# A linear-attention and Mish feed-forward kernel: the first feed-forward product by one level of Strassen's method, in two passes over DFF, with a written order on every engine

## The chip, the cores and the metric

The kernel runs on one core of a Trainium2 chip. The metric is device time in microseconds (us) of one execution, the median of several. Engines: PE (TensorE, matrix products), DVE (VectorE), ACT (ScalarE), POOL (GpSimd), and SP, whose queue issues all DMA transfers here.

## The reference

```python
def phi(x):
    proj = np.einsum('bhsd,df->bhsf', x, w_phi)
    proj = proj - np.max(np.abs(proj), axis=-1, keepdims=True)
    return np.concatenate([np.exp(proj), np.exp(-proj)], axis=-1)
q_p, k_p = (phi(q), phi(k))
kv = np.einsum('bhsf,bhsd->bhfd', k_p, v)
z = np.sum(k_p, axis=2)
num = np.einsum('bhsf,bhfd->bhsd', q_p, kv)
den = np.einsum('bhsf,bhf->bhs', q_p, z)[..., None] + 1e-06
attn_out = num / den
x = attn_out.transpose(0, 2, 1, 3).reshape(B * S, H * D)
h = x @ w_in
g = h * np.tanh(log1p(exp(h)))
out = g @ w_out
```

Batch 8, 8 heads, 576 positions, head width 64, 128 features; so x has 4608 tokens (rows) of DM = 512, and DFF = 2048. All is float32; `w_in` and `w_out` arrive as float64 words, of which the kernel makes float32 pairs.

## The kernel before, in words

**Attention.** The work is cut into 36 units of 512 rows each for k and for q. For a unit of k: a DMA brings it (`k_load`, L131), PE projects it (`project`, L103, 16 matmuls), DVE takes the largest magnitude of each row and subtracts it (L112, L113), ACT takes two exponentials (L147, L148), PE sums the products with v into PSUM (`k_sum`, L150), and ACT copies finished sums out (L163). For a unit of q: the same projection and subtraction, then PE transposes (`q_turn`, L176), ACT takes the exponentials out of PSUM (L182), PE multiplies with the sums of k (`q_num`, L184), DVE divides (L198 to L200), PE transposes back (`q_out`, L203), ACT copies (L211) and a DMA writes x to DRAM (`x_spill`, L212). k runs three units ahead of q (`LEAD`).

**Feed-forward.** Each float32 operand is split into a high part that PE's float32r format holds exactly and a low part; a product is three matmuls (high by high, high by low, low by high). x comes in 18 chunks of 256 tokens. A tile is 128 of DFF for one chunk: `ff_in` (L231) makes 12 matmuls of 128x256 (4 blocks of DM by 3), ACT applies Mish to two tiles at once (L251) and casts the high part (`gh`, L254), DVE subtracts for the low part (`gl`, L255), and `ff_out` (L259) makes 6 matmuls of 128x512 into two PSUM banks. There are 18 x 16 = 288 tiles.

**Weights.** They are split in 32 pieces of 128x512 by `split_weight` (L78): one ACT operation for the magnitude (L87), seven DVE operations (L89 to L94, L99, L100) and one ACT cast (L98). Sixteen pieces are split beside the attention and sixteen after it. The first four chunks are worked with half of DFF at a time (`NSPLIT`), so that the second sixteen have time.

**Order.** Each step is put in a list with a due time (`at`, L292) and emitted in order of these times. Inside `tc.manual_schedule(engines={PE})` (L343) only PE keeps the order of emission; the other engines and the DMA queue are put in order by a scheduler. `table` (L60) ties the ACT operations that need an activation table to each other. PSUM: `ps_a` holds two tiles of two banks (projections, later `h`), `ps_b` four tiles of one bank.

Of the kernel before, what the change touches and what calls it, by code (L numbers as in the profile page):

```python
# [38 lines left out]
def attention_then_mish(ctx, tc, qT, kT, va, w_phi, w_in, w_out, out):  # L39
# [18 lines left out]
    last = None

    def table(act):  # L60

        nonlocal last
        if last is not None:
            tc.add_manual_dep(act.ins, last.name, mybir.DependencyInfo(mybir.DependencyClass.NoSync, mybir.DependencyReason.DATA),
                              reason="table")
        last = act.ins


    weight, words_of = {}, {}

    def load_weight(pool, kind, i, j):
        nm = f"{kind}_{i}_{j}"
        src = w_in[i * P:(i + 1) * P, j * 512:(j + 1) * 512] if kind == "in" else w_out[i * P:(i + 1) * P, :]
        words = pool.tile([P, 1024], U32, tag=f"w{nm}", name=f"words_{nm}", bufs=1)
        nc.sync.dma_start(words, src.bitcast(U32))
        words_of[kind, i, j] = words.rearrange("p (a b) -> p a b", b=2)

    def split_weight(pool, kind, i, j):  # L78


        nm = f"{kind}_{i}_{j}"
        words = words_of.pop((kind, i, j))
        low, high = words[:, :, 0], words[:, :, 1]
        w = ffn.tile([P, 512], U32, tag="u", name=f"w_{nm}", bufs=3)
        t = ffn.tile([P, 512], F32, tag="t", name=f"t_{nm}", bufs=2)
        wf = w.bitcast(F32)
        nc.scalar.activation(wf, high.bitcast(F32), AF.Abs)  # L87

        nc.vector.tensor_scalar(wf, wf, LARGE, SMALL, op0=ALU.min, op1=ALU.max)  # L89
        nc.vector.tensor_scalar(w, w, 3, 0x3FFFFFF8, op0=ALU.logical_shift_left, op1=ALU.bitwise_and)  # L90
        nc.vector.scalar_tensor_tensor(w, high, 0xC0000000, w, op0=ALU.bitwise_and, op1=ALU.bitwise_or)

        nc.vector.tensor_scalar(t.bitcast(U32), w, 0xFF800000, None, op0=ALU.bitwise_and)
        nc.vector.scalar_tensor_tensor(t, low, 2.0 ** -52, t, op0=ALU.mult, op1=ALU.mult)  # L94
        parts = pool.tile([P, 2, 512], F32R, tag=f"w{nm}", name=f"parts_{nm}", bufs=1)
        hi, lo = parts[:, 0, :], parts[:, 1, :]
        weight[kind, i, j] = (hi, lo)
        nc.scalar.copy(hi, wf)  # L98
        nc.vector.tensor_sub(wf, wf, hi.bitcast(F32))  # L99
        nc.vector.tensor_tensor(lo, wf, t, op=ALU.add)  # L100


    def project(raw, name):  # L103

        ps = ps_a.tile([P, 2, 4, F], F32, tag="pp", name=f"pp_{name}")
        for n in range(4):
            for j in range(2):
                rows = slice(j * D, (j + 1) * D)
                nc.tensor.matmul(ps[:, j, n], raw[rows, n * P:(n + 1) * P], w_phi2[rows], start=True, stop=True)  # L109
# [34 lines left out]

    def k_exp(n):
        e = k_live[n]
        table(nc.scalar.activation(e[:, :, 1, :], e[:, :, 0, :], AF.Exp))  # L147
        table(nc.scalar.activation(e[:, :, 0, :], e[:, :, 0, :], AF.Exp, scale=-1.0))  # L148

    def k_sum(n):  # L150
        es = k_live.pop(n)
        for i in range(4):
            for p, slot in pairs_of(4 * n + i):
# [7 lines left out]
                if slot == 4:  # L161
                    kv[p // NHP, p % NHP] = att.tile([P, 2, 2, VW], F32, tag="kv", name=f"kv_{p}", bufs=10)
                    nc.scalar.copy(kv[p // NHP, p % NHP], kv_ps.pop(p))  # L163
# [214 lines left out]
```

## Time and profile before

| | |
|---|---|
| median of 3 runs | 1198.48 us (1198.43 to 1201.16) |
| profiled execution | 1201.74 us, of which the span of the profile is 1200.0 us |
| busy in the span | PE 1122.3, DVE 471.0, ACT 458.7, POOL 0.7 us |
| mean granted PE clock | 0.974 |
| DMA traffic | 78.43 MB |

The profile is one execution. A row of its windows view gives, for a stretch of the span, the busy time of each engine with the number of its instructions, then the granted PE clock (1.00 is full speed), the share of the DMA engines and GB/s. A row of the groups gives a line of the kernel, engine and operation, output and input with shapes and count, the busy time and the mean of one in ns, and the idle time of the engine ahead of them with what ended it. A row of the timeline gives start, length, engine, line and operation.

### The profile page before, as it was taken

To read this page: it belongs to the slowest core of one execution; us is meant where nothing else is said; L and a number is where in the kernel's file an instruction comes from. 1 tells how busy PE (TensorE), PEld (TensorE's weight loads), DVE (VectorE), ACT (ScalarE), POOL (GpSimd) and SP (SyncE) were. 2 spreads that over 40 slices of the span, in tenths; PEclk is the share of its full clock that TensorE was granted. 3 is DMA by queue.
4 is the path that set the end of the run, shared out by engine and by line. 5 is a ranking of instruction groups with operands and counts; after the bars stand their busy time and mean duration, and the time that the engine had idled before them with its cause. 6 is when DMAs were issued, how large, how long until landed. Compare 5 with 4: busy or idle time off the path is not lost.

```text
span 1200.0 us, 25819 instructions
## 1 busy us (share of the span) xinstructions
PE 1122.3 (94%) x11632; PEld 1017.9 (85%) x11632; DVE 471.0 (39%) x772; ACT 458.7 (38%) x708; POOL 0.7 (0%) x6
## 2 busy tenths in 40 slices
PE   5548899999999878999999999999999999999998
PEld 5548788888889777999999999999999999999997
DVE  7997677777753777222111111111111111111111
ACT  4445555656554777222222222222222222222221
POOL 0000000000000000000000000000000000000000
PEclk8779999999999989999999999999999999999999
DMA  9314444443313500111010010010010010000000
GB/s 364 129 39 132 142 157 128 137 133 124 114 55 138 205 19 18 36 54 36 19 36 19 18 36 18 19 36 19 18 36 18 19 36 19 18 19 1 19 18 18
DMA packets 33373, 78.43 MB, mean 65 GB/s; under 512 B 3696, under 2 KB 3824, under 8 KB 33264
## 3 DMA queue, kind: packets, MB, share of 16 engines
q1 hardware_dynamic: 33264, 76.79, 18.7%
q8 instruction: 91, 1.49, 0.5%
q14 instruction: 18, 0.15, 0.0%
HBM read 57.90 MB, written 18.87 MB: 64 GB/s over the span
## 4 chain that ended last, share of the span: by engine, by line
PE 72%; DVE 19%; ACT 3%; DMA 3%; issue 2%; SPq 1%; DVEq 0%; ACTq 0%
PE h L243 32%; PE o L273 31%; PE dt L180 3%; DVE e_q L113 3%; DVE m_k L112 3%; DVE e_k L113 3%; PE pp_k L109 3%; DVE m_q L112 3%; DMA words_out<-w_out 2%; PE num L121 1%; DVE x L200 1%; ACT L251 1%; PE kvps L121 1%; DMA x<-x_spill 1%; PE pp_q L109 1%
## 5 line engine op out<-in xcount | busy, mean ns | idle before, releaser
L243 PE MATMUL h<-xTh,parts_in 128*128 128x256 f32 x2304 | 459.2, 284 | 15.0 <-ACT u L251 15.0
L243 PEld LDWEIGHTS h<-xTh,parts_in 128*128 128x128 f32 x2304 | 378.2, 192 | 28.7 <-ACT u L251 17.5
L273 PE MATMUL o<-parts_out,gh 128*128 128x512 f32 x1152 | 363.6, 397 | 0.0
L243 PE MATMUL h<-xTl,parts_in 128*128 128x256 f32 x1152 | 326.9, 284 | 0.0
L255 DVE TENSOR_TENSOR gl<-u,gh 128x512 fp32r<-128x512 f32 x144 | 99.5, 691 | 486.5 <-ACT gh L254 486.4
L251 ACT ACTIVATE u<-h 128x512 f32<-128x512 f32 x144 | 86.1, 598 | 517.2 <-PE h L243 517.1
L243 PEld LDWEIGHTS h<-xTl,parts_in 128*128 128x128 f32 x1152 | 221.1, 192 | 10.0
L273 PE MATMUL o<-parts_out,gl 128*128 128x512 f32 x576 | 224.8, 390 | 0.0
L273 PEld LDWEIGHTS o<-parts_out,gh 128*128 128x128 f32 x1152 | 201.2, 191 | 27.7
L273 PEld LDWEIGHTS o<-parts_out,gl 128*128 128x128 f32 x576 | 109.1, 189 | 24.9
L121 PE MATMUL kvps<-v,e_k 128*64 128x65 f32 x2560 | 87.6, 230 | 4.0 <-ACT e_k L148 4.0
L254 ACT CAST gh<-u 128x512 fp32r<-128x512 f32 x144 | 89.4, 621 | 3.8
L121 PEld LDWEIGHTS kvps<-v,e_k 128*64 128x64 f32 x2560 | 82.6, 145 | 9.1 <-ACT e_k L148 4.6
L182 ACT ACTIVATE e_q<-dt 128x512 f32<-128x512 f32 x144 | 74.7, 603 | 12.7 <-PE dt L180 12.3
L121 PE MATMUL num<-kv,e_q 128*64 128x65 f32 x2304 | 74.3, 221 | 0.8 <-ACT kv L163 0.7
L180 PE MATMUL dt<-ident,e_q 128*128 128x128 f32 x288 | 45.6, 286 | 29.4 <-DVE r L198 17.9
L121 PEld LDWEIGHTS num<-kv,e_q 128*64 128x64 f32 x2304 | 70.8, 137 | 1.7 <-ACT kv L163 0.8
L112 DVE TENSOR_REDUCE m_k<-pp_k 128x8 f32<-128x1024 f32 x36 | 44.1, 1225 | 61.1 <-PE pp_k L109 61.1
L180 PEld LDWEIGHTS dt<-ident,e_q 128*128 128x128 f32 x288 | 31.8, 144 | 41.2 <-PE xt L209 13.4
L147 ACT ACTIVATE e_k<-e_k 128x1024 f32<-128x1024 f32 x36 | 38.1, 1057 | 72.2 <-DVE e_k L113 72.2
L228 DVE TENSOR_TENSOR xTl<-x,xTh 128x1024 fp32r<-128x1024 f32 x22 | 27.0, 1226 | 96.9 <-ACT xTh L227 96.9
L109 PE MATMUL pp_k<-w_phi,kraw 64*128 64x128 f32 x576 | 48.4, 315 | 11.5 <-issue 7.4
...
## 6 DMA issues: line engine op xcount, KB each, us to landing
...
kraw<-kT SPq DMA_DIRECT2D x36, 256.0 KB, 2.7
qraw<-qT SPq DMA_DIRECT2D x36, 256.0 KB, 3.2
x_spill<-xs SPq DMA_DIRECT2D x36, 256.0 KB, 2.0
out<-osb SPq DMA_DIRECT2D x36, 256.0 KB, 2.0
...
```

What stands on the lines that cost most here:

```text
L109: nc.tensor.matmul(ps[:, j, n], raw[rows, n * P:(n + 1) * P], w_phi2[rows], start=True, stop=True)
L112: nc.vector.tensor_reduce(m, ps, axis=AX.X, op=ALU.max, apply_absolute_value=True)
L113: nc.vector.tensor_tensor(e[:, :, 0, :].rearrange("p j (n f) -> p j n f", f=F), ps, m.unsqueeze(3).broadcast_to([P, 2, 4, F]), op=ALU.subt ...
L121: nc.tensor.matmul(ps[rows], lhsT[:, rows], rhs[h], start=start, stop=stop, skip_group_check=True)
L147: table(nc.scalar.activation(e[:, :, 1, :], e[:, :, 0, :], AF.Exp))
L180: nc.tensor.transpose(ps[:, i * P:(i + 1) * P], e[:, 0, i * P:(i + 1) * P], ident)
L182: table(nc.scalar.activation(e[:, s, :], ps, AF.Exp, scale=2.0 * s - 1.0))
L243: nc.tensor.matmul(ps, w[:, wcol], x[:, cc, :], start=(n == 0), stop=(n == 11))
L251: table(nc.scalar.activation(u, hv, AF.Mish))
L254: nc.scalar.copy(gh.rearrange("p f s -> p (f s)"), u)
L255: nc.vector.tensor_sub(gl.rearrange("p f s -> p (f s)"), u, gh.rearrange("p f s -> p (f s)").bitcast(F32))
L273: nc.tensor.matmul(ps, g[:, cols], w, start=(i == first and k == 0), stop=(i == end and k == 2))
```

## The change

**Strassen.** x comes in 9 chunks of 512 tokens, DFF in 8 blocks of 256, so there are 72 steps (`steps`). For one step the first product is a 2x2 block product (two blocks of 128 of DFF, two halves of DM, two halves of the tokens). Winograd's form of Strassen's method makes it from seven block products in place of eight: 7 products x 2 blocks of 128 in DM x 3 = 42 matmuls of 128x256. Four sums of weight blocks are made once for each weight piece (`sums`, on DVE), four sums of x blocks for each chunk that is loaded (`x_sum`, on POOL), and the seven products are put together by DVE and ACT (`first_product`, `winograd`). The second product is as before: 24 matmuls of 128x512 for a step. `ff_in` is in two parts: four products, then three that go into or beside the same banks, after DVE and ACT have read what the first four left.

**Two passes.** DFF is worked in two halves. Of the 32 weight pieces 8 are split beside the attention and 24 during the feed-forward; those of the second half (`fp` 4 to 7) are written to DRAM when split and read back once the place of the first half is free (`again`, `again_out`). Partial outputs go to DRAM (`o_part`) and come back (`part_load`).

**Engines.** `gl` is made on POOL, but for the last step. After the attention the magnitude of a weight is taken on DVE (`quiet`), not on ACT. `tc.manual_schedule()` now keeps the written order on all engines and on the DMA queue; `table` is gone. Steps that were one function are cut (`k_center`, `k_store`, `q_exp`, `q_norm`, `q_store`) so that each engine's part has a due time of its own. k runs four units ahead.

```diff
+PRODUCTS = ((0, 0, 0, 0), (4, 1, 0, 1), (3, 2, 1, 0), (5, 3, 1, 1), (2, 4, 0, 0), (6, 5, 1, 0), (1, 6, 1, 1))
...
+    def weight_ops(kind, fp, k, quiet):
...
+            if quiet:
+                nc.vector.tensor_scalar(w().bitcast(U32), words[:, 1], 0x7FFFFFFF, None, op0=ALU.bitwise_and)
+            else:
+                nc.scalar.activation(w(), words[:, 1].bitcast(F32), AF.Abs)
...
+        def sums(i):
...
+            nc.vector.tensor_tensor(o, x, y, op=op)
+
+        def hi():
...
+            nc.scalar.copy(dst[:, 0], piece[key][1][:, 1:8] if kind == "in" else w())
+
+        def lo():
+            dst = piece[key][3]
+            nc.vector.tensor_sub(dst[:, 1], piece[key][1][:, 1:8], dst[:, 0].bitcast(F32))
+            done()
...
+            if fp >= HALF:
+                nc.sync.dma_start(in_spill[fp, k] if kind == "in" else out_spill[fp, k], dst.bitcast(F32))
...
+    def x_sum(s, i):
...
+        nc.gpsimd.tensor_tensor(o, a, b, op=ALU.subtract)
+
+    def x_block(s, b):
...
+        nc.scalar.copy(blk[:, 0], src)
+        nc.vector.tensor_sub(blk[:, 1], src, blk[:, 0].bitcast(F32))
...
+    def ff_in(n, which):
...
+        for i in range(4) if which == 0 else range(4, 7):
+            wb, xb, bank, half = PRODUCTS[i]
+            ps = h_live[n][:, bank, half]
...
+                for w, x in ((wh, xh), (wh, xl), (wl, xh)):
+                    nc.tensor.matmul(ps, w, x, start=(i in (0, 2) and m == 0), stop=(m == 5), skip_group_check=True)
...
+        nc.scalar.copy(p1, h_live[n][:, 0, 0])
...
+            nc.vector.tensor_tensor(u2, ps[:, 0, 1], u_live[n][0], op=ALU.add)
...
+            nc.vector.tensor_tensor(u4, ps[:, 1, 0], u_live[n][1], op=ALU.add)
...
+            nc.vector.tensor_tensor(u[:, 3], ps[:, 1, 1], u_live[n][2], op=ALU.add)
...
+            nc.vector.tensor_tensor(u[:, 1:3], ps[:, 1], u2.unsqueeze(1).broadcast_to([P, 2, CH]), op=ALU.add)
...
+            nc.scalar.activation(u[:, 0], h_live[n][:, 0, 0], AF.Mish)
...
+            nc.scalar.activation(u[:, 1:4], u[:, 1:4], AF.Mish)
...
+        nc.scalar.copy(gh, u_live[n][3])
...
+        eng = nc.vector if n == len(steps) - 1 else nc.gpsimd
+        eng.tensor_tensor(gl, u_live.pop(n)[3], g_live[n][0].bitcast(F32), op=ALU.subtract)
...
+    segs = [(sc, (0, 1)) for sc in range(NFIRST)] + [(sc, (2, 3)) for sc in range(NFIRST)]
+    segs += [(sc, (0, 1, 2, 3)) for sc in range(NFIRST, NSC)] + [(sc, (4, 5, 6, 7)) for sc in range(NSC)]
...
-    with tc.manual_schedule(engines={mybir.EngineType.PE}):
+    with tc.manual_schedule():
```

**Where instructions moved.** First, DVE early in the attention. `m` and `e` are the largest magnitude and the difference of a unit; `w_`, `t_`, `words_` and `parts_` belong to weight pieces, and the last number of a name is that of its buffer. Before:

```order
L99 TENSOR_TENSOR w_out_0_1191<-w_out_0_1191,parts_out_0_1199 128x512
L91 SCALAR_TENSOR_TENSOR w_out_0_1771<-words_out_0_1345,w_out_0_1771 128x512
L99 TENSOR_TENSOR w_in_0_1481<-w_in_0_1481,parts_in_0_1489 128x512
L100 TENSOR_TENSOR parts_out_0_1199<-w_out_0_1191,t_out_0_1192 128x512
L112 TENSOR_REDUCE m_k_257<-pp_k_247 128x8
L100 TENSOR_TENSOR parts_in_0_1489<-w_in_0_1481,t_in_0_1482 128x512
L93 TENSOR_SCALAR t_out_0_1772<-w_out_0_1771 128x512
L89 TENSOR_SCALAR w_in_0_2059<-w_in_0_2059 128x512
L113 TENSOR_TENSOR e_k_256<-pp_k_247,m_k_257 128x2x512
```

The same engine now, at the units of the first weight piece (`r`, `num`, `x`: the division for a unit of q):

```order
L199 TENSOR_REDUCE m_q_601<-pp_q_493 128x8
L200 TENSOR_TENSOR e_q_600<-pp_q_493,m_q_601 128x2x512
L123 SCALAR_TENSOR_TENSOR w_in_0_543<-words_in_0_408,w_in_0_543 128x512
L129 TENSOR_SCALAR t_in_0_622<-w_in_0_543 128x512
L199 TENSOR_REDUCE m_k_652<-pp_k_631 128x8
L200 TENSOR_TENSOR e_k_651<-pp_k_631,m_k_652 128x2x512
L133 SCALAR_TENSOR_TENSOR t_in_0_622<-words_in_0_408,t_in_0_622 128x512
L145 TENSOR_TENSOR w_in_0_543<-w_in_0_543,t_in_0_622 128x512
L304 TENSOR_SCALAR r_0_547<-num_0_509 128x4
```

Before, operations of several pieces stood between the two operations of one unit; now one piece is worked at a time, two operations between the groups of a unit. The first weight operation is the 19th on DVE, behind five units of k and three of q.

Second, PE in the feed-forward. Before, the end of one tile's `h`, the `o` of an earlier tile, and the start of the next `h` (`parts_in`, `parts_out`: split weights):

```order
L243 MATMUL h_4_8061<-xTl_0_7862,parts_in_1_4371 128x256
L243 MATMUL h_4_8061<-xTh_0_7861,parts_in_1_4371 128x256
L273 MATMUL o_0_0_8110<-parts_out_0_1199,gh_0_8013 128x512 x2
L273 MATMUL o_0_0_8110<-parts_out_0_1199,gl_0_8014 128x512
L273 MATMUL o_0_1_8111<-parts_out_0_1199,gh_0_8013 128x512 x2
L273 MATMUL o_0_1_8111<-parts_out_0_1199,gl_0_8014 128x512
L243 MATMUL h_4_8061<-xTh_0_7861,parts_in_1_2644 128x256
```

Now, in a step n: the last matmul of an `o` for step n-1, four products (`xc_0` to `xc_3`, the x blocks), and the start of `o` for the other half of the tokens:

```order
L434 MATMUL o_1_7435<-wout_5482,gl_7372 128x512
L369 MATMUL h_7454<-xc_0_7388,win_832 128x256 x6
L369 MATMUL h_7454<-xc_1_7391,win_832 128x256 x6
L369 MATMUL h_7454<-xc_2_7395,win_832 128x256 x6
L369 MATMUL h_7454<-xc_3_7418,win_832 128x256 x6
L434 MATMUL o_2_7493<-wout_5482,gh_7368 128x512 x2
L434 MATMUL o_2_7493<-wout_5482,gl_7372 128x512
```

Tiles of 12 and 6 matmuls have become stretches of 24 (four products), 12 (`o` for step n-2, second half of the tokens), 18 (three products) and 12 (`o` for step n-1, first half). `gl` is needed by the third matmul of an `o`, right behind the two of `gh`.

Third, DVE while weights are split in the feed-forward. Before, with `gl` among them:

```order
L89 TENSOR_SCALAR w_out_0_5543<-w_out_0_5543 128x512
L255 TENSOR_TENSOR gl_1_5530<-u_1_5527,gh_1_5529 128x512
L90 TENSOR_SCALAR w_out_0_5543<-w_out_0_5543 128x512
L91 SCALAR_TENSOR_TENSOR w_out_0_5543<-words_out_0_5455,w_out_0_5543 128x512
L93 TENSOR_SCALAR t_out_0_5544<-w_out_0_5543 128x512
L94 SCALAR_TENSOR_TENSOR t_out_0_5544<-words_out_0_5455,t_out_0_5544 128x512
```

Now, from step 4 into step 5 (`u` from `h` are the `winograd` rows; `xc` is the low part of an x block):

```order
L133 SCALAR_TENSOR_TENSOR t_in_0_5709<-words_in_0_5595,t_in_0_5709 128x512
L145 TENSOR_TENSOR w_in_0_5688<-w_in_0_5688,t_in_0_5709 128x512
L381 TENSOR_TENSOR u_5_5742<-h_5712,p_5_5739 128x256
L385 TENSOR_TENSOR u_5_5746<-h_5712,u_5_5742 128x256
L389 TENSOR_TENSOR u_5762<-h_5712,u_5_5746 128x256
L353 TENSOR_TENSOR xc_0_5766<-x_3_5632,xc_0_5766 128x512
L353 TENSOR_TENSOR xc_1_5769<-xs_3_5664,xc_1_5769 128x512
L353 TENSOR_TENSOR xc_2_5773<-xs_3_5664,xc_2_5773 128x512
```

On POOL, which had nothing there, `gl` of two steps now stands between the sums of x blocks (`xs`) of one chunk and the next:

```order
L344 TENSOR_TENSOR xs_2_5448<-x_2_5417,xs_2_5448 128x512
L411 TENSOR_TENSOR gl_5521<-u_5438,gh_5517 128x1024
L411 TENSOR_TENSOR gl_5641<-u_5535,gh_5637 128x1024
L344 TENSOR_TENSOR xs_3_5664<-x_3_5632 128x512
L344 TENSOR_TENSOR xs_3_5664<-x_3_5632,xs_3_5664 128x512
```

`gl` has left DVE; in its place DVE has four `winograd` operations for a step and, in the last step of a chunk, seven x blocks, with weight operations in between.

More of the change, by code (lines that the diff above doesn't have):

```diff
@@ L47, in attention_then_mish @@
     att = att_scope.enter_context(tc.tile_pool(name="att", bufs=2))
+    late = None
     nc.scalar.preload_act_table_set("natural_log_exp_and_others")
@@ L56, in attention_then_mish @@
     x_spill = [tc.dram_tile([P, NCC, CH], F32, name=f"x_spill_{c}") for c in range(NCH)]
[L58 to L100, printed above, removed]
+    o_part = [tc.dram_tile([P, 4, DM], F32, name=f"o_part_{c}") for c in range(NSC)]
@@ new lines, in part_load, with ff_out @@
+    def part_load(s, sc):
+        part_live[s] = late.tile([P, 4, DM], F32, tag="part", name=f"part_{s}", bufs=2)
+        if seen_before[s]:
+            nc.sync.dma_start(part_live[s], o_part[sc])
+    def ff_out(n, which):
+        s, sc, fp, first, last = steps[n]
+        gh, gl = g_live[n]
+        assert not any(("out", fp, k) in pieces_left for k in range(2))
+        if first and which == 0:
+            o_live[s] = [None] * 4
+        for tt in (2 * which, 2 * which + 1):
+            if first:
+                o_live[s][tt] = ps_b.tile([P, DM], F32, tag="b", name=f"o_{s}_{tt}")
+            ps = o_live[s][tt]
+            cols = slice(tt % 2 * P, (tt % 2 + 1) * P)
+            for f in range(2):
+                wh, wl = wout[fp][:, f, 0], wout[fp][:, f, 1]
+                h, l = gh[:, 2 * f + which, cols], gl[:, 2 * f + which, cols]
+                for k, (g, w) in enumerate(((h, wh), (h, wl), (l, wh))):
+                    nc.tensor.matmul(ps, g, w, start=(first and f == k == 0), stop=(last and f == 1 and k == 2))
+        if which:
+            del g_live[n]
@@ new lines, in drain @@
+    def drain(n, tt):
+        s, sc, fp, first, last = steps[n]
+        ps, o = o_live[s][tt], part_live[s][:, tt]
+        if seen_before[s]:
+            nc.vector.tensor_tensor(o, ps, o, op=ALU.add)
+        else:
+            nc.scalar.copy(o, ps)
+        if sc_last[s]:
+            nc.sync.dma_start(out[(4 * sc + tt) * P:(4 * sc + tt + 1) * P, :], o)
+        elif tt == 3:
+            nc.sync.dma_start(o_part[sc], part_live[s])
+    segs = [(sc, (0, 1)) for sc in range(NFIRST)] + [(sc, (2, 3)) for sc in range(NFIRST)]
@@ L290, in attention_then_mish @@
+    pieces_left = set(pieces)
     events = []
@@ new lines, in attention_then_mish @@
+    window, clock = 0, free[0][0]
+    for i, pc in enumerate(pieces):
+        if i == 4 * 2:
+            while free[window][0] < begin:
+                window += 1
+            clock = free[window][0]
+        at(clock - 9.0, weight_load, *pc)
+        for cost, op in weight_ops(*pc, i >= 4 * 2):
+            while clock + 0.5 * cost > free[window][1]:
+                window += 1
+                clock = free[window][0]
+            at(clock, op)
+            clock += cost
+    for s, (sc, fps) in enumerate(segs):
+        n = steps.index((s, sc, fps[0], True, fps[0] == fps[-1]))
+        t = t_of(n - 2) if n >= AHEAD + 2 else begin - (45, 20)[s]
+        at(t + 1.0, x_load, s, sc)
+        for i in range(4):
+            at(t + 5.5 + 1.2 * i, x_sum, s, i)
+        t = t_of(n - 1) if n >= AHEAD + 2 else begin - (30, 3.9)[s]
+        for b in range(7):
+            at(t + 3.5 + 0.8 * b, x_block, s, b)
```

361 lines of the change are left out of this document (242 added, 119 removed).

## Prediction

> **What bounds the kernel now.** I read the windows of the span first, then the groups, then the timeline of one attention unit and of two feed-forward tiles. In the windows (columns: PE, weight loads, DVE, ACT, POOL busy, PE clock, DMA share, GB/s):
>
> ```profile
> 0.00:30.00 30.00, 17.14 (x263) 15.82 (x265) 21.57 (x38) 13.83 (x18) 0.70 (x6) 0.89 0.96 364
> 30.00:60.00 30.00, 17.88 (x311) 16.55 (x309) 30.00 (x50) 14.33 (x23) 0.00 (x0) 0.71 0.40 129
> 60.00:90.00 30.00, 14.01 (x218) 12.65 (x218) 29.06 (x59) 14.89 (x24) 0.00 (x0) 0.75 0.13 39
> 240.00:270.00 30.00, 28.87 (x690) 26.42 (x688) 22.34 (x34) 17.29 (x28) 0.00 (x0) 1.00 0.45 133
> 390.00:480.00 90.00, 75.02 (x436) 66.02 (x435) 67.09 (x124) 69.14 (x89) 0.00 (x0) 0.92 0.21 81
> 900.00:1000.00 100.00, 100.00 (x640) 90.92 (x639) 16.11 (x22) 24.78 (x40) 0.00 (x0) 1.00 0.06 22
> ```
>
> PE is the bound from 480 us on, and nearly so in the later attention. From 30 to 90 us DVE is full and PE works little, at a clock near 0.73: the scheduler has put the first sixteen weight pieces there. From 390 to 480 us PE does 436 matmuls; at the rate of the last row (640 in 100 us) they take 68 us, so 22 us are lost there, while the second sixteen are split.
>
> PE's pace comes from two places in the timeline. One attention unit:
>
> ```profile
> 241.45 2.55 PE L121 MATMUL kvps<-v,e_k 128*64 128x65 f32 x80
> 243.83 2.04 PE L121 MATMUL num<-kv,e_q 128*64 128x65 f32 x64
> 245.80 0.66 PE L209 MATMUL xt<-ident,x 128*128 128x128 f32 x4
> 246.57 1.37 PE L180 MATMUL dt<-ident,e_q 128*128 128x128 f32 x8
> 247.87 1.16 PE L109 MATMUL pp_k<-w_phi,kraw 64*128 64x128 f32 x16
> 248.86 1.06 PE L109 MATMUL pp_q<-w_phi,qraw 64*128 64x128 f32 x16
> ```
>
> and, with the rows between left out, two feed-forward tiles (24 matmuls of 256 columns, then 12 of 512):
>
> ```profile
> 701.71 0.28 PE L243 MATMUL h<-xTh,parts_in 128*128 128x256 f32 x1
> ...
> 704.59 0.63 PE L273 MATMUL o<-parts_out,gh 128*128 128x512 f32 x2
> ...
> 707.33 0.28 PE L243 MATMUL h<-xTh,parts_in 128*128 128x256 f32 x1
> ```
>
> From start to start a matmul of 256 columns takes 2.88/24 = 0.120 us, one of 512 columns 2.74/12 = 0.228 us. A tile of 12 and 6 is 2.81 us, and 288 tiles are 809 us. In the attention, start to start, a `kvps` matmul takes 2.38/80, a `num` 1.97/64, an `xt` 0.77/4, a `dt` 1.30/8 and a projection 0.99/16 us; the counts are 2560, 2304, 144, 288 and 1152, which makes 76 + 71 + 28 + 47 + 71 = 293 us, or 8.14 us a unit. PE's own work is 809 + 293 = 1102 us of the 1200 of the span. Of the 98 lost, 22 lie at 390 to 480 us; nearly all of the rest lies in the attention's first 120 us and at the two ends.
>
> The durations that the rest needs:
>
> ```profile
> L243 PE MATMUL h<-xTh,parts_in 128*128 128x256 f32 x2304 | 459.2, 284 | 15.0 <-ACT u L251 15.0
> L243 PE MATMUL h<-xTl,parts_in 128*128 128x256 f32 x1152 | 326.9, 284 | 0.0
> L112 DVE TENSOR_REDUCE m_k<-pp_k 128x8 f32<-128x1024 f32 x36 | 44.1, 1225 | 61.1 <-PE pp_k L109 61.1
> L113 DVE TENSOR_TENSOR e_k<-pp_k,m_k 128x1024 f32<-128x1024 f32 x36 | 44.1, 1225 | 2.7
> L198 DVE TENSOR_SCALAR r<-num 128x4 f32<-128x4 f32 x72 | 10.9, 152 | 5.5 <-PE num L121 5.2
> L199 DVE RECIPROCAL r<-r 128x4 f32<-128x4 f32 x72 | 12.6, 177 | 2.2
> L200 DVE TENSOR_TENSOR x<-num,r 128x256 f32<-128x256 f32 x72 | 30.4, 424 | 2.3
> L93 DVE TENSOR_SCALAR t_in<-w_in 128x512 uint32<-128x512 uint32 x16 | 6.8, 424 | 0.1
> L91 DVE SCALAR_TENSOR_TENSOR w_in<-words_in,w_in 128x512 uint32<-128x512 uint32 x16 | 11.0, 688 | 0.0
> L228 DVE TENSOR_TENSOR xTl<-x,xTh 128x1024 fp32r<-128x1024 f32 x22 | 27.0, 1226 | 96.9 <-ACT xTh L227 96.9
> L251 ACT ACTIVATE u<-h 128x512 f32<-128x512 f32 x144 | 86.1, 598 | 517.2 <-PE h L243 517.1
> L227 ACT CAST xTh<-x 128x1024 fp32r<-128x1024 f32 x22 | 22.9, 1042 | 10.2 <-DMA x<-x_spill 7.7 <-PE h L243 2.5
> L163 ACT COPY kv<-kvps 128x260 f32<-128x260 f32 x32 | 11.6, 362 | 10.9 <-PE kvps L121 10.9
> L251 ACT ACT_TABLE_LOAD x14 | 18.0, 1283 | 5.9 <-DVE parts_out L100 3.4 <-PE h L243 1.8 <-DVE parts_in L100 0.6
> L87 ACT ACT_TABLE_LOAD x12 | 15.4, 1283 | 1.5 <-DMA words_in<-w_in 1.3
> masks.py:199 POOL TENSOR_SCALAR_AFFINE_SELECT ident<-ident 128x128 f32<-128x128 f32 x1 | 0.3, 292 | 0.1
> ```
>
> **The change part by part.** *Strassen.* 3456 matmuls of `h` become 72 x 42 = 3024, the 1728 of `o` stay. A step is 42 x 0.120 + 24 x 0.228 = 10.52 us against four tiles of 2.81, so 72 steps are 757 us: 52 us go, all of it on PE, which is the bound there. This is the surest term.
>
> *Between the two parts of a step.* PE's second part adds to banks that DVE and ACT must have read. The first part ends at 2.88 us; ACT's copy of the first product (0.36, from L163) and the first sum (0.42, from L200) can run before that; two sums of 0.42 follow and end near 3.8. The second part starts behind 2.74 us of `o`, at 5.62. So 1.8 us of cover remain, and this costs nothing unless DVE is late.
>
> *`gl` on POOL.* ACT has ahead of it the copy (0.36), Mish of 768 columns (0.83, between 0.598 for 512 and 1.042 for 1024) and the cast of 1024 (1.04). It is free for that at 1.44, when the second product has ended, so `gl` starts near 3.9 with the handing over. The `o` that reads it begins at 2.88 + 2.74 + 2.16 = 7.78, its third matmul at 8.24: 4.3 us of room. POOL has no such operation in this trace. Bounds are 1.23 us (DVE's own 1024 columns, L228) and 8 x 0.292 = 2.34 us (POOL's 128 columns); I take 2.34, POOL's own row. It is hidden. The sums of x on POOL (4 x 1.17 us a chunk) have over ten us.
>
> *Attention.* PE's 293 us stay. DVE has for a unit 4 x 1.225 + 2 x (0.152 + 0.177 + 0.424) = 6.4 us. A piece of `w_in` now costs it 3 x 0.42 + 3 x 0.69, four sums of 128 columns (0.29 each, between 0.177 for 4 columns and 0.424 for 256) and a low part of 896 columns (1.09, between 0.69 and 1.226): 5.6 us; a piece of `w_out` 4.0. Four of each are 38 us, and the order spreads them over some 21 units, 1.8 us each. With about 0.4 us of handing over such a unit takes DVE 8.6 us, 0.5 more than PE's 8.14: 10 us. The division now also stands behind a weight operation, and PE's `xt` waits for it; with the other units near the 8.4 us of the timeline I put 17 us for the whole. The ends are 0 (all behind PE) and 45 (what the stretch from 30 to 90 us loses now).
>
> *Start and tail.* Four units of k run ahead with little for PE:
>
> ```profile
> 4.06 4.22 PE L109 MATMUL pp_k<-w_phi,kraw 64*128 64x128 f32 x32 [4.06 <-DMA kraw<-kT]
> 6.18 1.23 DVE L112 TENSOR_REDUCE m_k<-pp_k 128x8 f32<-128x1024 f32 x1 [6.18 <-PE pp_k L109]
> 12.25 3.74 PE L121 MATMUL kvps<-v,e_k 128*64 128x65 f32 x64 [3.97 <-ACT e_k L148]
> ```
>
> PE is slow then (2.1 us a projection against 0.99). Four projections and three `kvps` at that pace end near 24 us and are 10 us of work at full pace: 14 lost. At the end of the attention four units have no k; PE's 5.0 us each stand against a chain through all engines, filled by feed-forward steps 0 and 1. I put 6, between 0 and 12.
>
> *Weights in the feed-forward.* 24 pieces are split in steps 2 to 28. The ACT table loads go (26 of 1.28 us, since the magnitude moved to DVE at 0.42). In these 27 steps DVE has, by the rows above and the written order: weights 125 us, `winograd` 27 x 1.95 = 53, x blocks 77 of 0.69 = 53, partial sums 20 of 0.69 = 14; 245 in all. It also waits for ACT's cast inside a piece (24 x 0.9 = 22) and hands over some 500 times at 0.03 us (7.44 less the end of the row at 6.18): 15. That is 282 us against PE's 27 x 10.52 = 284. Steps 13 to 19 alone have over 11. Equal loads in a fixed order don't hide each other fully. The ends are 0 and 32 us (22 us for sixteen pieces, as at 390 to 480, times 24/16); I put 20.
>
> *DMA.* Weights, spilled pieces, x and partial outputs come to some 5 MB in two such steps, 240 GB/s against the 364 of the first window; in the last fifty steps far less. SP's queue is in written order, and a load behind a store that waits for DVE waits too; most loads are issued nine us or a step ahead. I count nothing; the 32 above covers it.
>
> *End.* The last partial sums (0.69) and a 2.0 us store stay: 4 us.
>
> ```profile
> out<-osb SPq DMA_DIRECT2D x36, 256.0 KB, 2.0
> ```
>
> The sum: 757 + 293 + 14 + 17 + 6 + 20 + 4 = 1111 us of span. The profiled execution is 1.7 us longer than its span, and 0.3% above the median; both together take off 1.6: 1110.
>
> **The rivals.** *POOL and DVE hold each other up* (1165 us). Most of DVE's work in steps 2 to 28 reads two SBUF operands, and so does POOL's. If one waits while the other reads, POOL's 27 x 2.34 + 40 x 1.17 = 110 us come on DVE's 282, less what runs beside DVE operations that read PSUM, some 33 (half of the 67 of `winograd` and partial sums): 359 against 284, so 75 lost in place of 20. The trace can't speak for or against: POOL's only work ends by 1.3 us, DVE's first row is at 6.18. [...]
>
> *The attention does not gain* (1145). If a fixed order stalls as often as the scheduler's did, the 37 us that I lose there (14 + 17 + 6) become the 72 of now (98 less 22 and 4).
>
> *Everything hides* (1077): no loss in steps 2 to 28, none in the tail, 10 in the attention.
>
> *POOL is slow* (1232, slower than before). Beyond 4.3 us of `gl`, PE waits in each of 72 steps for all that is over. At 5.5 us the gain is gone (72 x 1.2 = 86); at 6.0 us the time is 1110 + 122 = 1232. Against it stands the 0.292 row; for it, that this row is another operation with one input.
>
> **How the numbers follow.** Chances: the forecast 0.42, held up by POOL 0.36, no gain in the attention 0.10, everything hidden 0.08, POOL slow 0.04. A measurement of this kernel tells about 0.3% from no change. Only the last rival is slower; with 0.01 for something near 1198, faster has 0.95. The range leaves out POOL slow, most of what hides everything, and the far end of the second rival: 1085 to 1182.
>
> **What would show it.** After step 28 a step should take 10.5 us on PE, without gaps; else the first term is wrong. In steps 2 to 28, DVE rows longer than now, or DVE waiting beside a running POOL row, speak for the second rival; DVE without gaps and of the same lengths for the forecast. The first 120 us should show PE at 8 to 9 us a unit. A `gl` row above 4.3 us, with `o` waiting for POOL, would make the prediction wrong.

## The result, and the profile after

The changed kernel takes 1140.28 us (median of 4 runs, 1136.82 to 1145.88) against 1199.82 before (4 runs, 1198.43 to 1201.57): a ratio of 0.951, with an interval of 0.946 to 0.955. The profiled execution took 1138.37 us and its span is 1136.6, where the sum of the prediction came to 1111. So 25 us are to be found.

The page's lines on busy time, on the chain that ended last, and on the first product of PE:

```profile
PE 1064.7 (94%) x11200; PEld 964.7 (85%) x11200; DVE 750.4 (66%) x1178; ACT 493.7 (43%) x811; POOL 299.8 (26%) x169
...
PE 47%; DVE 20%; issue 3%; ACT 2%; DMA 1%; POOL 0%; DVEq 0%; ACTq 0%; SPq 0%; POOLq 0%
...
L369 PE MATMUL h<-xc,win 128*128 128x256 f32 x3024 | 397.5, 288 | 46.0 <-DVE u L389 45.4
```

DVE holds a fifth of the chain that ends last, and PE stood idle 45 us before `h` until DVE's third sum (L389) was there. The windows tell where (PE, weight loads, DVE, ACT, POOL busy, PE clock, DMA share, GB/s):

```profile
0.00:30.00 30.00, 20.98 (x411) 19.79 (x413) 15.25 (x13) 12.64 (x14) 0.70 (x6) 1.00 0.48 147
30.00:270.00 240.00, 236.58 (x5466) 220.13 (x5462) 221.17 (x376) 160.44 (x257) 5.03 (x4) 1.00 0.50 160
270.00:330.00 60.00, 50.65 (x715) 44.44 (x713) 34.65 (x67) 29.44 (x55) 10.17 (x6) 0.97 0.26 84
330.00:660.00 330.00, 284.34 (x1675) 253.54 (x1674) 298.64 (x428) 133.06 (x225) 127.77 (x69) 0.94 0.44 152
720.00:1100.00 380.00, 380.00 (x2389) 344.68 (x2388) 146.22 (x239) 127.45 (x212) 133.16 (x73) 1.00 0.28 100
```

The attention, from 30 to 270 us, now runs with PE busy for 237 of 240 us at full clock; before, it had stood half idle in part of it. The last row is the settled pace: 2389 matmuls in 380 us, 6.29 a microsecond, so 10.50 us for the 66 of a step. From 330 to 660 us, while the weights are split, the 1675 matmuls would take 266 us at that pace. 64 us are lost there: PE stands still for 46, and its matmuls take 18 us more than they need, at a granted clock of 0.94.

DVE is busy there for 299 of 330 us. Its groups of that stretch alone:

```profile
L353 DVE TENSOR_TENSOR xc<-x,xc 128x512 fp32r<-128x512 f32 x31 | 32.2, 1064 | 10.4 <-ACT xc L352 10.4
...
L123 DVE SCALAR_TENSOR_TENSOR w_out<-words_out,w_out 128x512 uint32<-128x512 uint32 x11 | 14.6, 1328 | 0.3
L145 DVE TENSOR_TENSOR w_in<-w_in,t_in 128x512 f32<-128x512 f32 x12 | 13.8, 1152 | 0.4
...
L119 DVE TENSOR_SCALAR w_in<-w_in 128x512 uint32<-128x512 uint32 x12 | 13.0, 1080 | 0.3
...
L389 DVE TENSOR_TENSOR u<-h,u 128x256 f32<-128x256 f32 x26 | 11.0, 425 | 2.7
```

Operations of kinds that took 0.69 us before the change (L353, L123, L145) take 1.06 to 1.33 on average, and L119, of a kind at 0.42 before, takes 1.08. These are among the rows stretched most: the 43 low parts that are made from sums of x (L353, `xc<-xs`) keep 0.68. L389, which reads a PSUM operand, keeps its 0.42. The timeline of DVE and POOL in one step shows what the long rows have in common:

```profile
412.41 2.75 POOL L411 TENSOR_TENSOR gl<-u,gh 128x1024 fp32r<-128x1024 f32 x1 [10.13 <-ACT gh L405]
412.82 2.63 DVE L110 TENSOR_SCALAR w_out<-words_out 128x512 uint32<-128x512 uint32 x1
415.13 1.48 POOL L344 TENSOR_TENSOR xs<-x 128x512 f32<-128x512 f32 x1
415.48 1.41 DVE L115 TENSOR_SCALAR w_out<-w_out 128x512 f32<-128x512 f32 x1
416.69 1.35 POOL L344 TENSOR_TENSOR xs<-x,xs 128x512 f32<-128x512 f32 x1
416.92 1.40 DVE L119 TENSOR_SCALAR w_out<-w_out 128x512 uint32<-128x512 uint32 x1
```

Each DVE row begins beside a POOL row and ends 0.28 or 0.29 us behind its end; three operations of 0.42 us take 5.4. And POOL's own groups, the first two from 290 to 660 us, the other two after it:

```profile
L411 POOL TENSOR_TENSOR gl<-u,gh 128x1024 fp32r<-128x1024 f32 x27 | 67.6, 2502 | 205.9 <-ACT gh L405 144.5 <-DMA x<-x_spill 14.5 <-DVE w_in L115 14.1
L344 POOL TENSOR_TENSOR xs<-x 128x512 f32<-128x512 f32 x24 | 36.0, 1500 | 43.7 <-DVE x L306 24.9 <-DMA x<-x_spill 18.8
...
L411 POOL TENSOR_TENSOR gl<-u,gh 128x1024 fp32r<-128x1024 f32 x44 | 105.7, 2403 | 306.3 <-ACT gh L405 306.3
L344 POOL TENSOR_TENSOR xs<-x 128x512 f32<-128x512 f32 x20 | 25.8, 1291 | 0.7 <-DMA x<-x_spill 0.7
```

POOL is held too, by 0.10 us a `gl` and 0.21 a sum of x.

### The profile page after: what moved, and what is told of

It reads as the page before. It is cut to its first block, busy times and chain, and to the rows that moved or that the text cites. A ratio compares the mean times of both kernels' runs of the same rounds, so it can differ in the third digit from the quotient of the medians.

```text
span 1136.6 us, 25710 instructions
## 1 busy us (share of the span) xinstructions
PE 1064.7 (94%) x11200; PEld 964.7 (85%) x11200; DVE 750.4 (66%) x1178; ACT 493.7 (43%) x811; POOL 299.8 (26%) x169
## 4 chain that ended last, share of the span: by engine, by line
PE 47%; DVE 20%; issue 3%; ACT 2%; DMA 1%; POOL 0%; DVEq 0%; ACTq 0%; SPq 0%; POOLq 0%
PE h L369 24%; PE o L434 23%; DVE xc L353 2%; DVE w_in L152 2%; DVE w_in L145 1%; DVE w_in L119 1%; DVE u L393 1%; DVE t_in L133 1%; DVE w_out L123 1%; DVE w_in L123 1%; DVE wst_in L161 1%; DVE u L385 1%; DVE u L389 1%; DVE w_out L110 1%; DVE t_in L129 1%
## 5 line engine op out<-in xcount | busy, mean ns | idle before, releaser
L369 PEld LDWEIGHTS h<-xc,win 128*128 128x128 f32 x3024 | 390.5, 196 | 61.6 <-issue 18.1
L369 PE MATMUL h<-xc,win 128*128 128x256 f32 x3024 | 397.5, 288 | 46.0 <-DVE u L389 45.4
L434 PE MATMUL o<-wout,gh 128*128 128x512 f32 x1152 | 362.0, 396 | 2.9 <-ACT gh L405 2.9
L411 POOL TENSOR_TENSOR gl<-u,gh 128x1024 fp32r<-128x1024 f32 x71 | 173.3, 2441 | 512.2 <-ACT gh L405 450.8
L434 PEld LDWEIGHTS o<-wout,gh 128*128 128x128 f32 x1152 | 210.4, 192 | 39.8 <-ACT gh L405 3.1
L434 PE MATMUL o<-wout,gl 128*128 128x512 f32 x576 | 226.0, 392 | 1.9 <-POOL gl L411 1.7
L344 POOL TENSOR_TENSOR xs<-x 128x512 f32<-128x512 f32 x46 | 64.4, 1399 | 307.3 <-DMA x<-x_spill 282.4
L434 PEld LDWEIGHTS o<-wout,gl 128*128 128x128 f32 x576 | 109.4, 190 | 27.4 <-POOL gl L411 3.2
L353 DVE TENSOR_TENSOR xc<-x,xc 128x512 fp32r<-128x512 f32 x69 | 75.0, 1114 | 23.9 <-ACT xc L352 23.9
L405 ACT CAST gh<-u 128x1024 fp32r<-128x1024 f32 x72 | 75.6, 1050 | 2.2
L353 DVE TENSOR_TENSOR xc<-xs,xc 128x512 fp32r<-128x512 f32 x92 | 63.2, 718 | 1.0 <-ACT xc L352 1.0
```

The costliest lines, as they stand in the source:

```text
L344: nc.gpsimd.tensor_tensor(o, a, b, op=ALU.subtract)
L353: nc.vector.tensor_sub(blk[:, 1], src, blk[:, 0].bitcast(F32))
L369: nc.tensor.matmul(ps, w, x, start=(i in (0, 2) and m == 0), stop=(m == 5), skip_group_check=True)
L405: nc.scalar.copy(gh, u_live[n][3])
L411: eng.tensor_tensor(gl, u_live.pop(n)[3], g_live[n][0].bitcast(F32), op=ALU.subtract)
L434: nc.tensor.matmul(ps, g, w, start=(first and f == k == 0), stop=(last and f == 1 and k == 2))
```

## The experiments

Theory A is the second rival of the prediction: POOL and DVE hold each other up. Theory B is that DVE's own work, in a fixed order, is too much for steps 2 to 28, with long rows only a symptom. *Lost* in the table is what PE loses between 330 and 760 us: 430 less the matmuls of that window over 6.29 a microsecond. *Held* is the sum over DVE's groups of that window, of the count times the mean length less the length in e1, where POOL does nothing (for DVE's sums of x and its `gl`, which e1 lacks, 0.685 and 1.225 us, as in e8). (e4 and e7 have other steps, e6 another attention; they aren't in these columns.)

| kernel | us, median | ratio to before, interval | lost | held |
|---|---|---|---|---|
| after | 1140.28 | 0.951, 0.946 to 0.955 | 64 | 87 |
| e1, POOL idle | 1074.51 | 0.896, 0.893 to 0.899 | 3 | 0 |
| e2, POOL fills, no waits | 1078.97 | 0.900, 0.897 to 0.902 | 3 | 0 |
| e3, DVE takes POOL's work | 1128.10 | 0.941, 0.939 to 0.943 | 53 | 6 |
| e4, eighth product | 1179.34 | 0.983, 0.980 to 0.986 | | |
| e5, POOL fills in place | 1075.13 | 0.896, 0.894 to 0.898 | 4 | 5 |
| e6, written order on PE alone | 1290.13 | 1.075, 1.072 to 1.078 | | |
| e7, e1 with eighth product | 1122.83 | 0.936, 0.934 to 0.938 | | |
| e8, e3 spread | 1129.93 | 0.942, 0.940 to 0.943 | 58 | 0 |
| e9, after spread | 1121.45 | 0.935, 0.933 to 0.936 | 48 | 90 |
| e10, gl earlier | 1137.25 | 0.948, 0.946 to 0.951 | 64 | 75 |
| e11, spread, gl earlier, sums on DVE | 1107.18 | 0.923, 0.921 to 0.925 | 33 | 37 |
| e12, e11 with gl behind the copy | 1106.97 | 0.922, 0.920 to 0.924 | 33 | 54 |

**e1: POOL does nothing.**

```diff
-        nc.gpsimd.tensor_tensor(o, a, b, op=ALU.subtract)
+        pass
-        src = (x32[:, 0:2, 0], ts[:, 1], ts[:, 0], ts[:, 2], x32[:, 2:4, 0], x32[:, 2:4, 1], ts[:, 3])[b]
+        src = (x32[:, 0:2, 0], x32[:, 2:4, 1], x32[:, 0:2, 1], x32[:, 2:4, 0], x32[:, 2:4, 0], x32[:, 2:4, 1], x32[:, 0:2, 1])[b]
-        eng.tensor_tensor(gl, u_live.pop(n)[3], g_live[n][0].bitcast(F32), op=ALU.subtract)
-        g_live[n].append(gl)
+        g_live[n].append(g_live[n][0])
```

> Left out: the low part of g (the third matmul of each pair reads gh instead of gl) and the four sums of x (blocks 1, 2, 3 and 6 are cut from x itself), so POOL does nothing after the identity; PE, ACT and the rest of DVE have the same instructions as after. Theory A, POOL and DVE hold each other up: DVE's rows of 330 to 660 us come back to their lengths in the attention (0.42 and 0.69 us; the stretch there adds up to 83 us), and the 63 us lost there fall to about the 20 of the forecast: 1095 us, 1080 to 1105. Theory B, DVE's own work in a fixed order is too much for steps 2 to 28 and the long rows are only where it happens to wait: the rows may be shorter, but the loss stays near 60: 1130 to 1140 us.

1074.51 us. In e1 the same stretch of the windows, and two of the groups of 330 to 630 us:

```profile
330.00:660.00 330.00, 328.39 (x2059) 296.26 (x2058) 240.39 (x466) 156.66 (x264) 0.00 (x0) 1.00 0.48 169
```

```profile
L145 DVE TENSOR_TENSOR w_in<-w_in,t_in 128x512 f32<-128x512 f32 x12 | 8.3, 692 | 0.4
...
L119 DVE TENSOR_SCALAR w_out<-w_out 128x512 uint32<-128x512 uint32 x12 | 5.1, 426 | 0.3
```

The rows are back at 0.69 and 0.42, PE works 328 of 330 us at full clock, and the loss is not 20 us but 3. Theory B falls: DVE's own load, weights included, fits beside PE's. Theory A stands, and the forecast's 20 us for loads that don't hide each other was too much. e1 also takes away the waits for what POOL makes, but they are no rival: in after, from 330 to 660 us, DVE has no idle time ahead of the low parts that read POOL's sums, and PE has 0.2 us ahead of the matmuls that read `gl`. In e5 below, what reads POOL's tiles still waits for POOL, and e5 is as fast as e1.

**e2 and e5: POOL writes and reads nothing.** In e2 the fills go to a spare tile; in e5 to the places of `gl` and of the sums.

```diff
-        nc.gpsimd.tensor_tensor(o, a, b, op=ALU.subtract)
+        nc.gpsimd.memset(o, 0.0)
-        eng.tensor_tensor(gl, u_live.pop(n)[3], g_live[n][0].bitcast(F32), op=ALU.subtract)
+        nc.gpsimd.memset(gl.bitcast(F32), 0.0)
```

> As e1, but in place of each low part and each sum of x POOL fills a spare tile of the same size with zeros: it writes SBUF and reads nothing. Theory A1, any work of POOL on SBUF holds DVE: rows that overlap a fill are stretched over it, and with fills as long as the subtractions the time is that of after, 1138 us; with shorter fills in proportion (0.2 us were measured for 128 columns, so some 1 to 1.6 us for 1024: 1110 to 1125). Theory A2, only POOL's reads hold DVE: rows at 0.42 and 0.69 us beside running fills, and the time of e1. Theory B: 1130 to 1140 in any case.

e2 didn't test what it was meant to: its fills wait for nothing that comes late, so POOL ran 120 of the 164 from 30 to 150 us, beside the attention, and the time (1078.97) says nothing on steps 2 to 28. But DVE splits eight pieces in the attention, and its groups there, from 30 to 150 us, are a test of another kind:

```profile
L119 DVE TENSOR_SCALAR w_in<-w_in 128x512 uint32<-128x512 uint32 x4 | 3.3, 814 | 0.1
L129 DVE TENSOR_SCALAR t_in<-w_in 128x512 uint32<-128x512 uint32 x4 | 3.1, 763 | 0.1
L145 DVE TENSOR_TENSOR w_in<-w_in,t_in 128x512 f32<-128x512 f32 x4 | 2.8, 692 | 0.1
...
L123 DVE SCALAR_TENSOR_TENSOR w_in<-words_in,w_in 128x512 uint32<-128x512 uint32 x4 | 2.7, 681 | 0.0
```

Operations with one SBUF input (L119, L129) are held, at 0.81 and 0.76 us on average where after has 0.43 in the same stretch; those with two (L145, L123) are not, at 0.69 and 0.68 in both.

> As after, but gl and the four sums of x are filled with zeros by POOL, in the places and with the waits that the subtractions have (so gl adds nothing to the output, and four of the seven blocks of x are zero). In e2 the fills waited for nothing and ran beside the attention: there rows of 0.42 us (one SBUF input) were stretched to 0.7 to 1.3 us beside a fill, rows of 0.69 us (two SBUF inputs) were not. Theory A2', a POOL instruction that only writes holds the one-input rows alone: in 330 to 660 us L115, L119 and L129 are longer than 0.42, L123, L133, L145 and L353 stay at 0.69, and since the one-input rows are 40 us of DVE's 216 the time stays near that of e1: 1075 to 1088. Theory A1, any POOL work holds every SBUF row: 52 us of fills, two thirds of them on DVE, 30 us lost, 1105.

1075.13 us, and e5 shows the same two kinds in the feed-forward (330 to 630 us). Its fills are not quite where the subtractions were: they wait for their place to come free (`gl` until PE's `o`), and not for `gh`.

```profile
L145 DVE TENSOR_TENSOR w_in<-w_in,t_in 128x512 f32<-128x512 f32 x12 | 8.3, 691 | 0.4
...
L119 DVE TENSOR_SCALAR w_in<-w_in 128x512 uint32<-128x512 uint32 x11 | 5.9, 540 | 0.3
L110 DVE TENSOR_SCALAR w_out<-words_out 128x512 uint32<-128x512 uint32 x12 | 5.9, 494 | 0.0
```

In e5 fills stretched only the one-input operations of 0.42 us, by 5 us in all in 69 us of POOL's work from 330 to 760 us; in after subtractions stretched these and the two-input ones, by 87 us in 160. So it is not POOL's work alone that holds the two-input operations: beside subtractions, which read two SBUF tiles, they were stretched, and beside fills, which read nothing, they were not; in e2 POOL was busy for 87 of the 120 us, and they kept their length. What in POOL and DVE makes this difference no run here shows. L389, which has one input in PSUM, stays at 0.42 in after and in e5.

**e3: DVE does POOL's work while weights are split.**

```diff
+        (nc.vector if s < 15 else nc.gpsimd).tensor_tensor(o, a, b, op=ALU.subtract)
+        eng = nc.vector if n < 29 or n == len(steps) - 1 else nc.gpsimd
```

> DVE itself computes gl of steps 0 to 28 and the sums of x of the first 15 segments; POOL does them only later. Theory A: DVE gets 27 x 1.23 + 24 x 2 x 0.69 = 66 us more and loses 83 us of stretch, its rows are at 0.42 and 0.69 us, and the 63 us lost fall by about 17: 1122 us, 1110 to 1135. Theory B: 66 us more on an engine that is already too full: about 1195 us.

1128.10 us, inside theory A's range: 66 us more on DVE cost a little less than 87 us of holding. Where both read SBUF, POOL as a helper was worth less than nothing here: after, with its help, takes 12 us more than e3. That the time fell so near 1122 is in part luck: the rows under e8 show that e3's loss is not the sum of DVE's work that the expectation was worked out from.

**e4 and e7: an eighth product.**

```diff
-        for i in range(4) if which == 0 else range(4, 7):
+        for i in range(4) if which == 0 else (4, 5, 6, 6):
```

> PE does the seventh product twice, 48 matmuls of h a step as before the change and not 42 (the last quarter of h is wrong by that product); everything else is as after. At 0.120 us a matmul this is 0.72 us a step. Theory A and B alike say that DVE and not PE sets the pace in steps 2 to 28, so that only the 45 other steps pay: 32 us, 1170. If PE sets the pace everywhere and Strassen's saving is had in full, 72 steps pay 52 us: 1190.

> e1 (no work on POOL, low part of g and sums of x left out) with the seventh product done twice. If PE sets the pace in every step once POOL is quiet, all 72 steps pay 0.72 us: 1074.5 + 52 = 1126 us. If DVE still has a share in steps 2 to 28, less: down to 1074.5 + 32 = 1107.

e4 takes 39 us more than after (1179.34 less 1140.28), e7 takes 48 more than e1 (1122.83 less 1074.51). With POOL quiet nearly all of the 52 us that Strassen's method saves on PE are there; in after 39 of them are, since part of the work that a step no longer has is replaced by waiting. e4 lies between its two values; e7 lies 3 us below the first of its two, 1126.

**e6: the written order on PE alone.**

```diff
-    with tc.manual_schedule():
+    with tc.manual_schedule(engines={mybir.EngineType.PE}):
```

> After, with the written order kept on PE alone and the other engines ordered by the scheduler, as before the change. If the attention's gain (72 us lost before by the prediction's count, 17 after) comes from the written order of DVE and ACT: DVE full and PE well below 29 of 30 us somewhere in the first 120 us, and 40 to 55 us more, 1180 to 1195. If it comes from the weights alone (8 pieces beside the attention and not 16): within 10 us of 1138.

1290.13 us, 95 us beyond the upper end of what was expected. In the attention it is as expected: from 30 to 150 us PE does 1699 matmuls where it does 2698 with the written order, and the last `num` begins at 387.0 us (311.4 in after, 368.9 before the change). What was not expected is that the feed-forward suffers as much, in steps without weights too:

```profile
30.00:150.00 120.00, 87.23 (x1699) 80.41 (x1695) 93.37 (x163) 56.43 (x88) 5.77 (x4) 0.82 0.42 138
...
760.00:1060.00 300.00, 280.72 (x1699) 250.16 (x1698) 110.64 (x162) 102.97 (x165) 102.28 (x54) 0.98 0.28 102
```

At 6.29 a microsecond the second row loses 30 of 300 us. Of these, 19 us are waits of PE until DVE's third sum; in after PE has none there. The timeline of e6 shows one of them:

```profile
902.69 3.04 PE L369 MATMUL h<-xc,win 128*128 128x256 f32 x24
...
905.76 0.38 ACT L374 COPY p<-h 128x256 f32<-128x256 f32 x1
...
906.27 1.28 DVE L353 TENSOR_TENSOR xc<-x,xc 128x512 fp32r<-128x512 f32 x2
...
907.47 0.41 DVE L381 TENSOR_TENSOR u<-h,p 128x256 f32<-128x256 f32 x1
...
907.81 0.67 DVE L353 TENSOR_TENSOR xc<-xs,xc 128x512 fp32r<-128x512 f32 x1
...
908.92 0.42 DVE L389 TENSOR_TENSOR u<-h,u 128x256 f32<-128x256 f32 x1
909.49 2.39 PE L369 MATMUL h<-xc,win 128*128 128x256 f32 x18 [1.02 <-DVE u L389]
```

ACT copies the first product 3.07 us into the step, as it does in after, so it is not ACT that is late. But DVE makes two low parts of x blocks ahead of the first sum and another behind it, and the third sum ends 6.65 us into the step (4.88 in a step of after that is shown further down). PE's second part waits for it. The written order is therefore no side matter of this change: with the scheduler's order on the other engines the same arithmetic is 7.5% slower than the kernel before.

**e8 and e9: the splitting spread to step 34**, with DVE doing POOL's work (e8) and with POOL doing it (e9).

```diff
-        if not steps[n][4]:
-            free.append((t_of(n) + 3.5, t_of(n) + 7.8))
-        free.append((t_of(n) + 8.9, t_of(n) + 11.9))
+        a, b = (7.8, 11.9) if n < 12 else (0, 11.3) if n < 20 else (7.0, 11.4)
+        if not steps[n][4] and a:
+            free.append((t_of(n) + 3.5, t_of(n) + a))
+        free.append((t_of(n) + 8.9, t_of(n) + b))
```

> e3 (DVE computes gl and the sums of x while weights are split) with the splitting spread to step 34: full windows to step 11, one window of 2.4 us a step to step 19, two of 6.0 us together from step 20; DVE does gl to step 35 and the sums of x of 14 segments. Theory A with DVE counted as in the prediction: in e3 it had 343 us for 27 steps of 284, 59 over and 54 lost; here 379 for 34 steps of 357, 22 over: 1128 - 32 = 1096 us, 1085 to 1110. If the loss in e3 came from the order (waits in series) and not from the sum of the work, spreading brings little: 1115 to 1130.

> After (gl and the sums of x on POOL) with the splitting spread as in e8. DVE's own work for the 34 steps is 317 us against 357; POOL has 34 x 2.40 + 56 x 1.29 = 154 us there, of which two thirds came on DVE in after (83 of 128): 100, so 417, 60 over where after had 81 over and lost 63: about 47 lost, 1123 us. If POOL's hold only hurts where DVE is full at that moment, the wider spread gains more: 1100 to 1110.

e9 gives 1121.45 where 1123 was expected: spread wider, the same 90 us of holding fall on steps with more room. e8 gives 1129.93 where 1096 was expected, and no holding at all. Its timeline shows what a sum of DVE's work leaves out:

```profile
476.13 0.42 DVE L385 TENSOR_TENSOR u<-h,u 128x256 f32<-128x256 f32 x1
476.41 1.05 ACT L405 CAST gh<-u 128x1024 fp32r<-128x1024 f32 x1
477.50 1.22 DVE L411 TENSOR_TENSOR gl<-u,gh 128x1024 fp32r<-128x1024 f32 x1 [0.95 <-ACT gh L405]
478.64 0.42 DVE L389 TENSOR_TENSOR u<-h,u 128x256 f32<-128x256 f32 x1
479.20 2.39 PE L369 MATMUL h<-xc,win 128*128 128x256 f32 x18 [1.23 <-DVE u L389]
```

`gl` moved to DVE at its old place in the order, between the second and the third sum. The third sum then waits for ACT's cast and for `gl`: it begins 6.45 us into the step (which starts at 472.19) where it begins at 4.46 in a step of after, and PE waits for it. In the whole run e8 has 34 waits of PE for the third sum, 46.3 us or 1.36 on average, and e3 has 26, 40.5 us or 1.56 on average. That this, and not the amount of work, is what keeps e3 and e8 from gaining is read from these rows; a kernel with `gl` on DVE behind the third sum was not run.

**e10: gl earlier.**

```diff
+        ahead = 1.5 if AHEAD <= n < len(steps) - 1 else 0.0
-        at(after + 0.9, mish, n, 1)
-        at(after + 1.8, g_hi, n)
-        at(after + 2.8, g_lo, n)
+        at(after + 0.9 - ahead, mish, n, 1)
+        at(after + 1.8 - ahead, g_hi, n)
+        at(after + 2.8 - ahead, g_lo, n)
```

> After with the same operations on the same engines, only ordered otherwise: from step 2 on the second part of Mish, the cast to gh and gl on POOL stand 1.5 us earlier, so that gl begins near 1.3 us of a step and runs beside DVE's three sums that read PSUM (1.5 to 3.3 us, rows that no run stretched), and not beside the weights' window that begins at 3.5. Theory A: of POOL's 128 us in 330 to 660 us the 66 of gl no longer fall on SBUF rows; the sums of x still do, 62 us, two thirds of them on DVE, 40. DVE's 282 + 40 = 322 against 284: about 30 of the 63 us lost remain, 1105 us, 1095 to 1115. If the loss came from POOL's amount of work and not from what it runs beside, nothing changes or ACT's earlier order costs something: 1138 to 1150.

1137.25 us: no gain to speak of, next to the 1138 that was put down for the other side. But the edit did not do what it was for, as the timeline of e10 shows:

```profile
406.80 2.40 POOL L411 TENSOR_TENSOR gl<-u,gh 128x1024 fp32r<-128x1024 f32 x1 [8.06 <-ACT gh L405]
406.91 2.57 DVE L129 TENSOR_SCALAR t_out<-w_out 128x512 uint32<-128x512 uint32 x1
...
410.12 0.42 DVE L381 TENSOR_TENSOR u<-h,p 128x256 f32<-128x256 f32 x1
```

`gl` started while DVE was still in the window of the step before, held one of its operations for all of its length, and that operation stands ahead of the three sums. Held time went from 87 to 75 us only: a place in the order fixes no time, and `gl` did not come to lie beside the sums that read PSUM.

**e11 and e12: the three remedies together.** e11 is e9 with e10's order, and with the sums of x of the first 14 segments on DVE. e12 is e11 with the cast to gh behind the copy of the first product:

```diff
-        at(after + 1.8 - ahead, g_hi, n)
-        at(after + 2.8 - ahead, g_lo, n)
+        at(after + 1.8 - 0.6 * ahead, g_hi, n)
+        at(after + 2.8 - 0.6 * ahead, g_lo, n)
```

> e10 with the splitting spread to step 34 as in e9 and the sums of x of the first 14 segments on DVE, so that POOL has nothing but gl beside the weights. DVE: 317 us for the 34 steps and 56 x 0.69 = 39, so 356 against 357, with next to nothing held: 0 to 20 us lost where after lost 63, 1075 to 1095 us; 1087. If the waits in series of e8 (third sum behind an operation that waits for ACT) return in this order: 1110 to 1130.

> e11 with one difference: ACT's cast to gh stands behind the copy of the first product and not ahead of it, so gl starts near 2.1 us of a step and not near 0. In e10 and e11 gl started while DVE still worked in the window of the step before: one row of it was held for 2.4 to 2.9 us, and that row stands ahead of the three sums that PE's second part waits for. Here the first of the three sums waits for the copy that stands ahead of the cast, so gl meets sums that read PSUM, and at most the first row of the next window for its last 1 to 1.5 us, behind the sums. If the place of the held row ahead of the sums is what is left of the loss: about 20 of the 32 us that e11 still loses from 330 to 660 us go, 1087 us, 1078 to 1098. If it is DVE's load (held time falls from 2.4 to some 1.3 us in 28 steps, PE's wait only in the steps where DVE is full): 1095 to 1105.

e11 takes 1107.18 us: 20 more than expected, between its two ranges, and 23 less than e8. That is 2.8 points of the time before below after (0.923 against 0.951, intervals in the table). e12 is no faster, 1106.97, above both of its ranges, although its order does what it was for:

```profile
402.07 0.42 DVE L381 TENSOR_TENSOR u<-h,p 128x256 f32<-128x256 f32 x1
402.31 2.40 POOL L411 TENSOR_TENSOR gl<-u,gh 128x1024 fp32r<-128x1024 f32 x1 [7.63 <-ACT gh L405]
...
403.06 0.42 DVE L389 TENSOR_TENSOR u<-h,u 128x256 f32<-128x256 f32 x1
403.40 1.86 DVE L166 TENSOR_TENSOR w_out<-w_out,wout 128x512 f32<-128x512 f32 x1
```

The sums now run beside `gl` at 0.42 us, and what is held stands behind them. So the place of the held operation ahead of the sums was not what is left. DVE is held for 54 us in e12, and busy for 282 of the 330 us to 660: with the sums of x on it, it is near its limit again. How the last 33 us divide between DVE's load, what is still held, and waits in series was not told apart.

## Why the prediction was right or wrong

The time lay in the range, 30 us above the forecast and 25 below the second rival; of the two, the rival had the cause, as the loss fell from 64 to 3 us with POOL idle (e1). The range holds the time because it was drawn to take in most of that rival, and because two misses of the forecast, 44 us too little in the weights and 20 too much in the attention, in part cancel.

*Strassen.* Right: 10.50 us a step against 10.52, and 48 of the 52 us come back when an eighth product is put in with POOL quiet.

*Between the two parts of a step.* The prediction gave 1.8 us of cover, and no cost "unless DVE is late". The cover was read wrong: it let ACT's copy and the first sum run before the four products end. A step of after:

```profile
406.69 3.04 PE L369 MATMUL h<-xc,win 128*128 128x256 f32 x24
...
409.76 0.37 ACT L374 COPY p<-h 128x256 f32<-128x256 f32 x1 [4.47 <-PE h L369]
...
411.15 0.42 DVE L389 TENSOR_TENSOR u<-h,u 128x256 f32<-128x256 f32 x1
...
412.31 2.32 PE L369 MATMUL h<-xc,win 128*128 128x256 f32 x18
```

The copy starts behind all four, at 3.07 us of the step (in e1 and in steps without weights too), the third sum ends at 4.88, and 0.7 us are left before the second part at 5.62. And DVE was late by more: 45 us of PE's waiting stand before `h`, until the third sum.

*`gl` and the sums of x.* The lengths were nearly right (2.40 unheld against 2.34; 1.29 against 1.17), which is luck, as they came from a row of another operation with one input. `gl` itself is hidden: PE's `o` waits for it 1.7 us in all.

*Attention.* The start lost 14 us as predicted: the 288 matmuls of `kvps` and 123 of the projections in the first 30 us are 16 us of work at the prediction's prices. The middle was to lose 17. Its 5466 matmuls of 30 to 270 us cost 248 us at those prices and ran in 240, so it gained 8: the 8.14 us a unit that were read as full pace contained waits. In after a unit takes 7.33 us (from 204.32 to 211.65), an `xt` group of it 0.50 where 0.77 was read and a `dt` group 0.96 where 1.30 was. The tail lost 11 where 6 were put, at 49 us of work in 60. Together 17 instead of 37. The rival by which the attention doesn't gain is answered by e6: without the written order it gains nothing.

*Weights in the feed-forward.* This is the step that failed: 20 us, with ends of 0 and 32, against 64. It took DVE's rows at the lengths of a trace in which POOL does nothing, and then put 20 us on imperfect hiding. e1 corrects both halves: with such rows there is nothing to lose, what was counted as 282 us fits beside 284 (3 us lost); with POOL reading beside them 87 us come on top. The term's ends should have held the second rival's 75, as nothing in the trace excluded it.

*The second rival's own sum.* Its 77 us of holding were 82 in the same stretch; POOL has 128 us there and not 110, since its rows are held as well (a sum of x took 1.51 us where 1.17 was put) and four more sums fall into it. 282 + 82 less 284 would lose 80; 64 were lost, so some of the holding lay in gaps of DVE's. The 33 us that the rival took off for DVE operations that read PSUM were an estimate that no run shows by itself; in after these operations kept their length (L389 0.42 us, the partial sums of L442 0.68).

*DMA* and *end* were as predicted: the tail from 660 us on loses 5 us (472 of work in 477), and the only DMA that PE waits for is the first load, 4.2 us.

The sum: 43 or 44 us more in the weights, 20 less in the attention, 1 more at the end, which is the 25 us between 1111 and 1136.6.
